# Moving the right-hand SBUF buffers of a float32r attention-and-two-MLPs kernel by 64 and 128 bytes

## The chip, the core and the metric

The kernel is one program on one core of a Trainium2 chip. The metric is the device time of one execution in microseconds (us); lower is better. The time before is 800.19 us, the median of three runs (800.11 to 800.76).

## The reference, cut to what matters

```
# attention over 32 memory slots, 4 batches x 8 heads, 576 rows, head size 64
a      = softmax(phi)                               # phi: b h 576 32
k_m, v_m = a^T k, a^T v                             # b h 32 64
attn   = softmax(q k_m^T / 8);  x = attn v_m        # x: 2304 x 512
# first MLP, d_ff 1536                                second MLP, d_ff 2048
y = ((x w_a) * (x w_b)) w_out                       out = elu(y w_in) w_out2     # 2304 x 512
```

The weights arrive as float64 and are rounded to float32 on the chip. A float32 product is done as three float32r products of a high and a low part each (high x high, high x low, low x high).

## The kernel before, in words

Everything stays in SBUF; TensorE (PE) runs one long, fixed stream of products. A "moving" operand streams through PE, a "stationary" operand is loaded ahead of it by a weight load (PEld). In the built program `matmul(out, w, x)` has `w` stationary and `x` moving. One weight load goes with every product.

The stages, in order:

- **Attention**, about the first 65 us: loads of phi, k, v and q, transposes, scores and softmax, in plain float32 (L376 to L493).
- **ab** (`steps_ab`, L625): 1152 float32r products, 288 columns each. Stationary is `u` (the memory values already multiplied by the weights, made by `step_u`, L513), moving are the attention weights `xhi`, `xlo`.
- **o1** (`steps_o1`, L652): 864 float32r products of 384 columns. Stationary are the weight parts `ulh`, `ull`, moving are the hidden values `gh`, `gl`. ab and o1 alternate from about 91 to 392 us. A run of o1 is 4 column blocks (`for c in range(KC)`), each over a list of hidden blocks `fs`, each with 3 pairs of parts x 2 halves. The last hidden block (the key `own`) has weight tiles of its own in another pool (`pb`, in `to_hi`).
- **h** (`step_h`, L750): 1152 float32r products of 384 columns; stationary `ush`, `usl`, moving `yh`, `yl` of one of three row blocks t = 0, 1, 2.
- **o2** (`steps_o2`, L795): 864 float32r products of 512 columns. Here the activations `g2h`, `g2l` (named `gh`, `gl` in the code) are stationary and the weights `ulh`, `ull` move. h and o2 alternate from 392 us to the end.

VectorE (DVE) and ScalarE (ACT) evacuate PSUM, split values in high and low parts, and convert the weights in pieces (`fill`) beside each step. GpSimd (POOL) issues weight loads, SyncE (SP) the rest.

Pools are taken from two sides of SBUF. Those opened with `side="right"` (`rim`, `py`, `p0`, `pl`, `pb`, `pd`) are stacked from the upper end downwards in the order in which they are opened, each tile in whole units of 32 bytes per partition; the others (`conv`, `pa`, `pu`, `pc`) from the lower end upwards. `edge` (L272) is the first tile at the right, so all tiles of the right side lie below it; `parity` (L292) lies in `p0`, below `y` and above what is opened later.

Of the kernel before, what the change touches and what calls it, by code (L numbers as in the profile page):

```python
# [7 lines left out]
F32 = mybir.dt.float32  # L8
# [13 lines left out]
def attention_then_two_mlps(ctx, tc, q, kv, kv_left, phi, w_ab, w_o1, w_i2, w_o2, out):  # L22
# [14 lines left out]
    B, P, KC, S = q.shape  # L37
# [233 lines left out]
    es_u = ExitStack()  # L271
    pu = es_u.enter_context(tc.tile_pool(name="pu", bufs=2, reuse_waits="tile"))  # L272
    rim = ctx.enter_context(tc.tile_pool(name="rim", bufs=1, side="right", reuse_waits="tile"))
    edge = rim.tile([P, 8], F32, name="edge")
    es_y = ExitStack()
    py = es_y.enter_context(tc.tile_pool(name="py", bufs=1, side="right", reuse_waits="tile"))
    y = [py.tile([P, KC * TB], F32, name=f"y{i}") for i in range(NB)]
# [3 lines left out]
    p0 = es_0.enter_context(tc.tile_pool(name="p0", bufs=2, side="right", reuse_waits="tile"))  # L281
# [7 lines left out]
    ident = p0.tile([P, P], F32, name="ident", bufs=1)  # L289
    rest = pl.tile([P, LEFT, 2], F32, name="rest", bufs=1)  # L290
    a_left = pl.tile([P, 2, P], F32, name="a_left", bufs=1)
    parity = p0.tile([P, 2], F32, name="parity", bufs=1)  # L292


    st = {}
# [599 lines left out]
```

## Time and profile before

| | |
|---|---|
| median of 3 runs | 800.19 us (800.11 to 800.76) |
| the profiled execution | 800.3 us, of which the span from first to last instruction is 798.6 us |
| TensorE's mean granted clock | 0.999 of full speed |
| PE / PEld busy | 779.9 us (98%) / 720.0 us (90%) |
| DVE / ACT busy | 588.9 us (74%) / 398.3 us (50%) |

The profile is one execution. PE's durations of single products overlap, since the products are pipelined; the pace of a stream is therefore read from the starts of its rows, or from a piece of the chain of waits divided by its count. The chain of waits follows the work that ended last back from the end.

### The profile page before, as it was taken

The numbers are of one execution on the slowest core, as the hardware profiler recorded it, in microseconds if no ns is written. First come the engines' busy times: TensorE is split into PE (matmuls) and PEld (weight loads), VectorE is DVE, ScalarE is ACT, GpSimd is POOL, SyncE is SP. The second block draws the span as 40 slices with busy tenths as digits, with TensorE's granted clock in tenths as the row PEclk, the third lists the DMA queues.
The fourth block names the chain that finished last, engine by engine and source line by source line (L and its number), as shares of the span: only waits on it lengthen the run. The fifth ranks groups of instructions, "written<-read, shape, count | busy, mean of one in ns | idle before, by whom it ended". The sixth has DMA issues, their size and how long they took to land.

```text
span 798.6 us, 12970 instructions
## 1 busy us (share of the span) xinstructions
PE 779.9 (98%) x5420; PEld 720.0 (90%) x5420; DVE 588.9 (74%) x924; ACT 398.3 (50%) x616; POOL 38.2 (5%) x83
## 2 busy tenths in 40 slices
PE   5899999999999999999999999999999999999997
PEld 4788899999999999999998988998889988999896
DVE  5798985887787787787997327777977779676464
ACT  5555774543363335333686536554565445653350
POOL 2000000000000000000000000000000000000000
PEclk9999999999999999999999999999999999999999
DMA  9960222121212221121001000111111111000006
GB/s 340 408 268 27 64 97 75 36 76 55 80 33 74 62 71 54 53 78 55 27 27 54 26 1 27 53 53 53 54 47 34 53 53 54 27 1 0 1 1 237
DMA packets 17066, 57.71 MB, mean 72 GB/s; under 512 B 1776, under 2 KB 1776, under 8 KB 17008
## 3 DMA queue, kind: packets, MB, share of 16 engines
q0 software_dynamic: 8784, 31.99, 12.4%
q1 hardware_dynamic: 8224, 24.91, 8.0%
q8 instruction: 42, 0.69, 0.3%
q14 instruction: 16, 0.13, 0.1%
HBM read 52.17 MB, written 4.72 MB: 71 GB/s over the span
## 4 chain that ended last, share of the span: by engine, by line
PE 91%; DMA 4%; DVE 3%; ACT 1%; issue 0%; SPq 0%; DVEq 0%; ACTq 0%
PE o_ps L795 25%; PE h_ps L750 25%; PE o_ps L652 18%; PE ab_ps L625 18%; DMA y<-in_q_dram 3%; PE u_ps L513 3%; PE sc L438 1%; DMA kv_t<-in_kv_dram 1%; DVE ssm L476 0%; PE pk L399 0%; DVE y L481 0%; DVE u L524 0%; PE tp_x L489 0%; DVE gl L636 0%; PE sl L442 0%
## 5 line engine op out<-in xcount | busy, mean ns | idle before, releaser
L625 PE MATMUL ab_ps<-xhi,u 128*128 128x288 f32 x768 | 138.2, 296 | 0.0
L625 PEld LDWEIGHTS ab_ps<-xhi,u 128*128 128x128 f32 x768 | 113.6, 188 | 6.0 <-ACT gh L635 3.7
L795 PE MATMUL o_ps<-ulh,g2h 128*128 128x512 f32 x288 | 113.7, 395 | 0.0
L795 PE MATMUL o_ps<-ull,g2h 128*128 128x512 f32 x288 | 113.6, 394 | 0.0
L770 DVE SCALAR_TENSOR_TENSOR e<-e,th 128x768 f32<-128x768 f32 x48 | 45.8, 954 | 78.4 <-ACT e L767 78.4
L795 PE MATMUL o_ps<-ulh,g2l 128*128 128x512 f32 x288 | 103.0, 395 | 0.0
L750 PE MATMUL h_ps<-yh,usl 128*128 128x384 f32 x384 | 97.8, 335 | 0.0
L750 PE MATMUL h_ps<-yl,ush 128*128 128x384 f32 x384 | 97.7, 335 | 0.0
L750 PE MATMUL h_ps<-yh,ush 128*128 128x384 f32 x384 | 97.6, 335 | 0.0
L761 ACT ACTIVATE e<-h_ps 128x768 f32<-128x768 f32 x48 | 38.9, 811 | 93.6 <-PE h_ps L750 93.1
L625 PE MATMUL ab_ps<-xlo,u 128*128 128x288 f32 x384 | 81.5, 294 | 0.0
L652 PE MATMUL o_ps<-gh,ulh 128*128 128x384 f32 x288 | 74.0, 338 | 0.6 <-ACT ulh L146 0.6
L652 PE MATMUL o_ps<-gh,ull 128*128 128x384 f32 x288 | 73.9, 338 | 0.0
L652 PE MATMUL o_ps<-gl,ulh 128*128 128x384 f32 x288 | 73.9, 337 | 0.0
L632 ACT ACTIVATE a_sb<-ab_ps 128x576 f32<-128x576 f32 x48 | 31.3, 653 | 79.8 <-PE ab_ps L625 79.8
L750 PEld LDWEIGHTS h_ps<-yh,ush 128*128 128x128 f32 x384 | 69.6, 188 | 1.3
L750 PEld LDWEIGHTS h_ps<-yh,usl 128*128 128x128 f32 x384 | 69.4, 188 | 0.0
L750 PEld LDWEIGHTS h_ps<-yl,ush 128*128 128x128 f32 x384 | 69.3, 188 | 0.0
L795 PEld LDWEIGHTS o_ps<-ulh,g2l 128*128 128x128 f32 x288 | 54.0, 187 | 13.2
L795 PEld LDWEIGHTS o_ps<-ulh,g2h 128*128 128x128 f32 x288 | 54.0, 187 | 12.6
L795 PEld LDWEIGHTS o_ps<-ull,g2h 128*128 128x128 f32 x288 | 54.0, 187 | 12.5
L634 DVE TENSOR_TENSOR a_sb<-a_sb,ab_ps 128x576 f32<-128x576 f32 x48 | 36.0, 752 | 36.8 <-PE ab_ps L625 36.4
(95 smaller groups left out, 1291.2 us busy)
## 6 DMA issues: line engine op xcount, KB each, us to landing
raw<-in_w_o_dram POOLq DMA_DIRECT2D x27, 512.0 KB, 3.8
raw<-in_w_ab_dram POOLq DMA_DIRECT2D x18, 512.0 KB, 3.8
kv_t<-in_kv_dram SPq DMA_DIRECT2D x16, 512.0 KB, 10.2
raw<-in_w_i_dram POOLq DMA_DIRECT2D x16, 512.0 KB, 3.8
y<-in_q_dram SPq DMA_DIRECT2D x8, 576.0 KB, 10.2
out_dram<-y SPq DMA_DIRECT2D x8, 512.0 KB, 2.9
raw<-in_w_ab_dram SPq DMA_DIRECT2D x6, 512.0 KB, 9.2
phi_t<-in_phi_dram SPq DMA_DIRECT2D x3, 576.0 KB, 9.9
```

The source lines that it names most:

```text
L438: nc.tensor.matmul(sc[:, u, j * P:(j + 1) * P], qs[u][:, t, j * P:(j + 1) * P], kt[:, u, t * P:(t + 1) * P], start=(t == 0), stop=(t == 1))
L513: nc.tensor.matmul(ps[j:j + M, o, k * 256:k * 256 + 256], vt[r, 2 * k + c, 2 * p + o], w[r, c * 256:c * 256 + 256], start=True, stop=True, ...
L625: nc.tensor.matmul(ps[:, h, 0:HS], u[:, kk, w, n * P:n * P + P], x[b][:, kk, h * HS:(h + 1) * HS], start=(kk == 0 and i == 0), stop=(kk == ...
L632: nc.scalar.activation(out=a_sb, in_=ps[:, :, 0:HS], func=AF.Copy)
L634: nc.vector.tensor_tensor(out=a_sb, in0=a_sb, in1=ps[:, :, 0:HS], op=ALU.mult)
L652: nc.tensor.matmul(ps[:, h, 0:HB], w[:, cc], g[:, h * HB:(h + 1) * HB], start=(n == 0 and i == 0), stop=(n == len(fs) - 1 and i == 2),)
L750: nc.tensor.matmul(ps[:, h, 0:HB], w[:, c], x[:, c, h * HB:(h + 1) * HB], start=(c == 0 and i == 0), stop=(c == KC - 1 and i == 2),)
L761: nc.scalar.activation(out=e, in_=ps[:, :, 0:HB], func=AF.Relu, scale=-1.0)
L770: nc.vector.scalar_tensor_tensor(out=e, in0=e, scalar=1.0, in1=th, op0=ALU.add, op1=ALU.mult)
L795: nc.tensor.matmul(ps[:, k, :], g[:, c * P:(c + 1) * P], w, start=(f == fs[0] and i == 0), stop=(f == fs[-1] and i == 2),)
```

## The change

`edge` grows from 8 to 24 float32 (32 to 96 bytes per partition), and `parity` becomes the first two columns of a tile of 34 (32 to 160 bytes with rounding). Tiles between the two (`y`, and the small softmax tiles, which lie below `y`) move down by 64 bytes, and all right-hand tiles under `parity` by 64 + 128 = 192.

```
-    edge = rim.tile([P, 8], F32, name="edge")
+    edge = rim.tile([P, 24], F32, name="edge")
...
-    parity = p0.tile([P, 2], F32, name="parity", bufs=1)
+    parity = p0.tile([P, 34], F32, name="parity", bufs=1)[:, 0:2]
```

No instruction is added, removed or moved on any engine; two become wider (the memset and the exponential of `edge`, 8 to 24 columns). What changes is where operands begin. The start addresses in the built programs, modulo 256 bytes, as (moving, stationary):

```
products                                count   before        after
ab  L625  xhi,xlo / u, first halves       576   (0|128, 128)  the same
ab  L625  xhi,xlo / u, second halves      576   (128|0, 128)  the same
o1  L652  gh,gl / ulh,ull                 792   (64, 128)     (128, 128)
o1  L652  the same, block "own"            72   (64, 64)      (128, 128)
h   L750  yh,yl / ush,usl, t = 0, 1       768   (128, 128)    the same
h   L750  the same, t = 2                 384   (192, 128)    (128, 128)
o2  L795  ulh,ull / g2h,g2l               864   (128, 192)    (128, 128)
attention, u (float32): ident/y (64,192)->(128,128); y/y (192,192)->(128,128);
  kv/a (64, 192|64)->(128, 0|128); pick in y/m (192,64)->(128,128); ush/vt: the same
```

In ab the two row halves of a product are 1152 bytes apart, so its moving operand alternates between 0 and 128; in the other streams a slice keeps the residue of its tile. Modulo 512 the moved right-hand tiles of o1, h and o2 begin at 384 afterwards, and the left-hand ones at 128, as before.

## Rows read from the trace of the kernel before

**Rows 1.** The page, busy time by engine, and the granted clock by slices.
```profile
PE 779.9 (98%) x5420; PEld 720.0 (90%) x5420; DVE 588.9 (74%) x924; ACT 398.3 (50%) x616; POOL 38.2 (5%) x83
PEclk9999999999999999999999999999999999999999
```

**Rows 2.** The page, chain of waits: shares by engine and by line.
```profile
PE 91%; DMA 4%; DVE 3%; ACT 1%; issue 0%; SPq 0%; DVEq 0%; ACTq 0%
PE o_ps L795 25%; PE h_ps L750 25%; PE o_ps L652 18%; PE ab_ps L625 18%; DMA y<-in_q_dram 3%; PE u_ps L513 3%; PE sc L438 1%; DMA kv_t<-in_kv_dram 1%; DVE ssm L476 0%; PE pk L399 0%; DVE y L481 0%; DVE u L524 0%; PE tp_x L489 0%; DVE gl L636 0%; PE sl L442 0%
```

**Rows 3.** Engines by stretch, from 110 us on; columns in the first row.
```profile
core 0: us, PE busy (x) PEld busy (x) DVE busy (x) ACT busy (x) POOL busy (x), PEclk, DMA share, GB/s
110.00:392.00 282.00, 282.00 (x2308) 273.61 (x2307) 218.10 (x368) 123.75 (x209) 17.40 (x32) 1.00 0.19 61
392.00:768.00 376.00, 376.00 (x1907) 341.22 (x1906) 263.10 (x365) 205.11 (x276) 12.63 (x23) 1.00 0.10 33
```

**Rows 4.** Waits of PE's weight loads after 110 us: total, times, longest.
```profile
PEld ab_ps L625 <- ACT gh L635: 3.7, 9, 0.4
```

**Rows 5.** The chain in order of time: start, us, what.
```profile
131.64 9.36 PE ab_ps L625 x72
...
152.81 12.71 PE o_ps L652 x72
...
376.45 3.18 PE ab_ps L625 x24
...
446.58 12.50 PE h_ps L750 x72
...
475.88 12.51 PE h_ps L750 x72
...
488.39 12.59 PE o_ps L795 x54
...
500.99 12.53 PE h_ps L750 x72
...
513.52 12.60 PE o_ps L795 x54
```

**Rows 6.** Timeline of PE, last o1 runs for t = 1 and 2.
```profile
379.48 0.51 PE L652 MATMUL o_ps<-gh,ulh 128*128 128x384 f32 x2
...
383.64 0.52 PE L652 MATMUL o_ps<-gh,ulh 128*128 128x384 f32 x2
...
384.70 0.51 PE L652 MATMUL o_ps<-gh,ulh 128*128 128x384 f32 x2
...
385.74 0.52 PE L652 MATMUL o_ps<-gh,ulh 128*128 128x384 f32 x2
```

**Rows 7.** Timeline of PE, last o1 run for t = 0: start, us, what.
```profile
363.69 0.51 PE L652 MATMUL o_ps<-gh,ulh 128*128 128x384 f32 x2
...
365.77 0.51 PE L652 MATMUL o_ps<-gh,ulh 128*128 128x384 f32 x2
...
366.81 0.52 PE L652 MATMUL o_ps<-gh,ulh 128*128 128x384 f32 x2
...
368.93 0.51 PE L652 MATMUL o_ps<-gh,ulh 128*128 128x384 f32 x2
...
369.97 0.52 PE L652 MATMUL o_ps<-gh,ulh 128*128 128x384 f32 x2
```

**Rows 8.** Timeline of PE, first and last pair of an early o1 stretch.
```profile
99.65 0.51 PE L652 MATMUL o_ps<-gh,ulh 128*128 128x384 f32 x2
...
105.55 0.51 PE L652 MATMUL o_ps<-gh,ull 128*128 128x384 f32 x2
```

**Rows 9.** The instructions on edge: min/median/max ns, first and last start.
```profile
L528 POOL MEMSET edge<- x1: 105/105/105, 0.7 to 0.7; 128x8 f32 x1
L529 ACT ACTIVATE edge<-edge x1: 209/209/209, 2.0 to 2.0; 128x8 f32<-128x8 f32 x1
```

**Rows 10.** The chain in order of time, its DMA pieces at the start.
```profile
2.58 6.51 DMA kv_t<-in_kv_dram
9.11 11.96 DMA y<-in_q_dram
21.09 9.76 DMA y<-in_q_dram
```

## The prediction

> **What bounds the kernel now.** I read the page first. PE is busy 98% of the span and its clock is granted in full, the 2.4 GHz level, in every slice [rows 1]. The chain of waits says that this busy time is also the path: PE holds 91% of it, and 86% is four streams of products, o2 25%, h 25%, o1 18%, ab 18% [rows 2]. The table by stretches shows that from 110 us to 768 us PE has no gap, while DVE is busy 218.1 of 282.0 us and ACT less [rows 3]; the waits of the weight loads in that time are nine of at most 0.4 us, all in ab, 3.7 us in total [rows 4]. So the time is a sum of counts times paces, and the reader must look at the pace, the time from one product's start to the next. The mean durations do not give it, since products overlap.
>
> The chain's pieces give the paces [rows 5]:
> - ab, 288 columns: 9.36 us / 72 = 130.0 ns.
> - h, 384 columns: 12.50, 12.51 and 12.53 us / 72 = 173.6 to 174.0 ns.
> - o1, 384 columns: 12.71 / 72 = 176.5 ns.
> - o2, 512 columns: 12.59 and 12.60 / 54 = 233.2 to 233.3 ns.
>
> h and o1 have the same number of columns and the same shapes, yet o1 is 2.5 to 2.9 ns slower. 130.0 / 288 = 0.451 ns per column, and 0.451 x 384 = 173.3: ab and h lie on one line, o1 lies over it. The same line at 512 columns gives 231.1, and o2 lies 2.2 ns over it. The two streams over the line are the ones whose moving address minus stationary address is 192 modulo 256. On the line are differences of 0 (h, t = 0 and 1) and 64 (h, t = 2); ab mixes 0 and 128.
>
> **Does the address do it?** The kernel holds its own experiment. In the last o1 runs the block "own" has its weights in the right-hand pool, so (64, 64) products stand between (64, 128) products of the same line, shape and time. For t = 1 there are 24 products at (64, 64), from 379.48 to 383.64 us: 4.16 us / 24 = 173.3 ns. Then come, for t = 2, six at (64, 128), from 383.64 to 384.70: 1.06 / 6 = 177; six at (64, 64) to 385.74: 1.04 / 6 = 173 [rows 6]. For t = 0, twelve at (64, 128) from 366.81 to 368.93 take 2.12 / 12 = 176.7, the next six at (64, 64) 1.04 / 6 = 173.3 [rows 7]. The pace follows the address pair, back and forth within a microsecond, and equal residues sit on the line.
>
> One thing speaks against a simple rule. The first twelve of that run, 363.69 to 365.77, are (64, 128) too and take 2.08 / 12 = 173.3 [rows 7], and in an early run the 34 products from 99.65 to 105.55 take 5.90 / 34 = 173.5 [rows 8]. So (64, 128) can run on the line if the stream enters it in step, and mostly does not; after each (64, 64) block it fell off again. I take the difference as something that makes the slow step possible, and equality as something that removes it.
>
> **The Trainium skill against this.** "TensorE: Matmul & The Clock Gate", section "Step-by-step: what each phase is for", says that PE reads its streaming operand and its weights through two independent ports, so loading the next weights takes no bandwidth from the running product. By it no start address would matter and the sum would be 0, 800.3 us in the profiled execution. The 177 and 173 ns of [rows 6] disagree.
>
> **The change part by part.**
> 1. o1 to (128, 128). Of 864 products, 72 are at (64, 64) already. Of the 792 at (64, 128), 12 are seen on the line in [rows 7], and 36 (those 34 and the last two) in the early run of [rows 8]. That leaves 744 x (176.5 - 173.3 = 3.2 ns) = 2.4 us. Bounds: 0, and 792 x 3.7 (the slowest six of [rows 6]) = 2.9.
> 2. o2 to (128, 128). 864 x (233.3 - 231.1 = 2.2 ns) = 1.9 us. No row shows 512 columns at equal residues; the 231.1 is an estimate, the line through ab and h. Bounds: 0 if 233.3 is what 512 columns take anyway, and 864 x 3.2 = 2.8 if o1's whole step goes. I take 1.9, because o2 has o1's difference of 192 and is over the line as o1 is.
> 3. h, t = 2, from (192, 128) to (128, 128): 0. Its pace is on the line now, and so is that of t = 0 and 1. The runs differ by 0.03 us [rows 5]; 16 steps of t = 2 give at most some 0.3 us either way.
> 4. ab and u have both operands on the left: 0. Attention's float32 products change residues, but before 65 us PE is not the limit; 0, and 0.5 us either way.
> 5. The exponential of `edge` (209 ns) and the memset (105 ns) get 16 more columns [rows 9]; both lie before 2.3 us, while the chain goes on with the k/v load until 9.1 us [rows 10]. 0. If the cover were gone, they could cost no more than their own length again, 0.3 us.
> 6. Loads into right-hand tiles move their SBUF address from 64 or 192 to 128. The chain holds 6.51 + 11.96 + 9.76 = 28.2 us of them [rows 10]. Nothing in the trace shows a load's price by address. The nearest rows are the two pieces for q, which differ by 2.2 us at one and the same residue, so the ends are 2.2 us either way; I take 0, since a move by whole 64 bytes changes neither the count nor the size of the packets.
>
> What is late next? PE stays the path: DVE has 282.0 - 218.1 = 64 us free where o1 gives 2.4, and the waits of [rows 4] are at most 0.4 us each, so at most a few tenths come back there.
>
> Sum: 2.4 + 1.9 = 4.3 us. The profiled execution took 800.3 (span 798.6 and 1.7 around it), 0.1 over the median of 800.19. 800.19 - 4.3 = 795.9 us.
>
> **The rivals.**
> - *Only o1 gains.* Then 233.3 ns belongs to 512 columns and not to the address. For: o2 holds the same 233.2 to 233.3 in both of its runs in [rows 5], whereas o1 shows two paces, and 512 is no multiple of 96 while 288 and 384 are, so a pace that goes by steps could round up. Against: o2 sits over the line with o1's difference. 800.19 - 2.4 = 797.8 us.
> - *Nothing changes.* The pace in o1 is set by the phase in which a stream begins, and the new pair, which lies 256 and not 0 apart modulo 512 (384 and 128), leaves o1 and o2 where they are. For: the same pair shows two paces [rows 7, 8]. Against: the switches within the last runs go with the address [rows 6, 7]. 800.2 us. The skill's rule above would give the same time.
> - *More.* o2's step goes whole (2.8), and h's runs of 12.51 and 12.53 all become 12.50 or less, some 0.5: 800.19 - 2.4 - 2.8 - 0.5 = 794.5 us.
> - *Slower.* Products at (384, 128) modulo 512 collide where none did. ab shows that a stream can get slower at unmoved addresses: 3.18 / 24 = 132.5 instead of 130.0 ns [rows 5], 1.9%. If h, t = 2, takes 1.9% more (384 x 3.3 = 1.3 us) and o2 too (864 x 4.4 = 3.8) while o1 stays, the time is 805.3; with h alone 801.5. It decides from the point where h and o2 lose 1.6 us more than o1 gives. Against: h at (128, 128) is on the line.
>
> **How the numbers follow.** Both o1 and o2 gain: 0.50 (795.9, its own range 795.2 to 796.8). Only o1: 0.25 (797.8, within 0.5). More: 0.07. Nothing: 0.11. Slower: 0.07. A measurement of this kernel can tell 0.2%, 1.6 us, from no change, so faster means under 798.6: the first three, 0.82. Same, 0.11; slower, 0.07. The range must take in the first two cases and most of the third: 794.6 to 798.5.
>
> **What would show it.** In the profile after, every o1 run of 72 in the chain should read 12.48 to 12.50 us instead of 12.71; o2's runs of 54 should read 12.48 instead of 12.60 (12.60 still, if only o1 gains); h for all t 12.50; ab 9.36 as now; the first 65 us the same within 0.5. The prediction is wrong if o1 still reads 12.7, or if ab or h grow.

## The result, and the profile after

The changed kernel takes 793.65 us, the median of five runs (793.42 to 794.12), against 800.19 before (five runs, 799.52 to 800.76): ratio 0.9918, 95% interval 0.9907 to 0.993. The direction was forecast; the size was not. The forecast was 795.9 us with a range from 794.6 to 798.5, and the time lies 0.95 us below the range.

The page of the changed kernel, busy time by engine, answers to [rows 1]:

```profile
PE 773.4 (98%) x5420; PEld 719.1 (91%) x5420; DVE 588.7 (74%) x924; ACT 398.2 (50%) x616; POOL 38.1 (5%) x83
```

PE's busy time fell by 6.5 us, and no other engine's by more than 0.9: the same work, at another pace. PE stays the path. In the table by stretches it has no gap (first fence, columns as in [rows 3]), and the waits of the weight loads in ab are again nine of at most 0.4 us, 3.7 in all (second fence, as [rows 4]):

```profile
110.00:392.00 282.00, 282.00 (x2312) 273.63 (x2311) 219.29 (x369) 123.64 (x209) 17.35 (x32) 1.00 0.19 61
392.00:768.00 376.00, 376.00 (x1926) 345.00 (x1925) 266.26 (x368) 207.69 (x280) 12.60 (x23) 1.00 0.10 33
```

```profile
PEld ab_ps L625 <- ACT gh L635: 3.7, 9, 0.4
```

The chain in order of time (start, us, what) answers to [rows 5]:

```profile
53.37 3.77 PE sc L438 x32
...
81.00 9.79 PE ab_ps L625 x72
...
130.83 9.59 PE ab_ps L625 x72
...
152.13 12.50 PE o_ps L652 x72
...
390.80 24.96 PE h_ps L750 x144
...
444.59 12.50 PE h_ps L750 x72
...
473.45 12.50 PE h_ps L750 x72
485.96 12.28 PE o_ps L795 x54
498.24 12.50 PE h_ps L750 x72
510.74 12.28 PE o_ps L795 x54
```

Per product, o1 went from 176.5 to 12.50 / 72 = 173.6 ns, o2 from 233.3 to 12.28 / 54 = 227.4, h is at 173.6 in its runs of 72, and ab right behind o1 went the other way, from 130.0 to 9.59 / 72 = 133.2. Three pieces of the chain of before, with those above, give the ledger:

```profile
53.95 3.77 PE sc L438 x32
...
81.59 9.79 PE ab_ps L625 x72
...
392.20 25.03 PE h_ps L750 x144
```

| stretch | before | after | less |
|---|---|---|---|
| start to 81 us (attention) | 81.59 | 81.00 | 0.6 |
| ab and o1, up to the first h | 310.6 | 309.8 | 0.8 |
| h, o2 and the end of the span | 406.4 | 401.1 | 5.3 |
| span | 798.6 | 791.9 | 6.7 |

Of the 5.3, o2 is 864 x 5.9 ns = 5.1. In the middle stretch o1 gave 2.2 us (nine runs of 12.71 now at 12.48 to 12.50, and two shorter steps), and ab took 1.5 back: 456 products stand directly behind an o1 run, at 3.3 ns more each.

### The profile page after: what moved, and what is told of

Its sections match the earlier page's. It is cut to its first block, busy times and chain, and to the rows that moved or that the text cites. A ratio compares the mean times of both kernels' runs of the same rounds, so it can differ in the third digit from the quotient of the medians.

```text
span 791.9 us, 12970 instructions
## 1 busy us (share of the span) xinstructions
PE 773.4 (98%) x5420; PEld 719.1 (91%) x5420; DVE 588.7 (74%) x924; ACT 398.2 (50%) x616; POOL 38.1 (5%) x83
## 4 chain that ended last, share of the span: by engine, by line
PE 90%; DVE 4%; ACT 1%; issue 0%; DVEq 0%; ACTq 0%
PE h_ps L750 25%; PE o_ps L795 25%; PE ab_ps L625 19%; PE o_ps L652 18%; PE u_ps L513 3%; PE sc L438 0%; DVE y L465 0%; DVE ssm L476 0%; DVE smx L464 0%; DVE a L181 0%; DVE y L481 0%; DVE u L524 0%; DVE gl L636 0%; DVE ush L201 0%; DVE xlo L70 0%
## 5 line engine op out<-in xcount | busy, mean ns | idle before, releaser
L795 PE MATMUL o_ps<-ulh,g2h 128*128 128x512 f32 x288 | 112.0, 389 | 0.0
```

The costliest lines, as they stand in the source:

```text
L795: nc.tensor.matmul(ps[:, k, :], g[:, c * P:(c + 1) * P], w, start=(f == fs[0] and i == 0), stop=(f == fs[-1] and i == 2),)
```

## The experiments

**One tile at a time.** Each half of the change alone.

```
 edge_only:    edge = rim.tile([P, 24], ...)          parity as before
 parity_only:  parity = p0.tile([P, 34], ...)[:, 0:2]   edge as before
```

Edge alone:

> The kernel before with the wider edge tile alone: y and all tiles below move by 64 bytes, so o2 stands at (128, 128), h for t = 2 at (128, 128), and o1 at (0, 128), a difference of 128. Theory A (a weight load costs a product a fixed 13.3 ns at equal residues, and a step of 3.3 or 6.7 ns more where the residues differ badly): o2 at 227.4 ns as with the whole change, which alone takes 864 x 5.9 = 5.1 us off; o1 has the difference of 128 at which ab shows both paces, so 173.4 to 176.7; total 792.7 to 795.1. Theory B (o2's pace fell for another reason than its own addresses, such as the state in which o1 leaves the stream): o2 stays at 233.3 and the total at 797.8 to 800.2.

Measured: 795.22 us against 799.92, ratio 0.9944 (0.993 to 0.9957). Chain of waits of that kernel:

```profile
130.67 9.60 PE ab_ps L625 x72
...
152.06 12.67 PE o_ps L652 x72
...
487.71 12.28 PE o_ps L795 x54
```

o2 has the whole of its new pace, 227.4 ns, from its own addresses: theory B is out. o1 at (0, 128) is at 12.67 / 72 = 176.0, hardly better than at (64, 128), and ab has lost its 130.0 all the same, so a fast o1 is not what slows ab. Theory A had no such loss in it; the total is 0.1 over its interval.

Parity alone:

> The kernel before with the wider parity tile alone: o1 stands at (192, 128), a difference of 64, its block own at (192, 192); o2 stays at (128, 192) and h as before. Theory A1 (a difference of 64 is as free as 0, as h at t = 2 showed before): o1 at 173.4 ns, 2.4 us less; ab after such an o1 run takes 9.59 us for 72 instead of 9.36, as with the whole change, up to 1.5 us more; total 797.8 to 799.3. Theory A2 (only equal residues are free): o1 at 176.5 and ab at 9.36; total 800.2. Both: o2 at 233.3.

Measured: 799.41 us, ratio 0.999 (0.9982 to 0.9999).

```profile
130.75 9.58 PE ab_ps L625 x72
...
152.13 12.48 PE o_ps L652 x72
...
487.00 12.59 PE o_ps L795 x54
```

A1: o1 at (192, 128), a difference of 64, runs at 12.48 / 72 = 173.3, as fast as at equal residues. A2 is out. ab pays for most of it, and o2 stays. The total is 0.1 over the interval that A1 gave.

So much for nine of the eleven late runs. In the last two, products at (192, 128) and those of "own" at (192, 192) take turns, and they read 12.58 and 12.60 us where before they read 12.61 and 12.56. From the timeline, the first six of "own" in the first of the two take 1.07 / 6 = 178 ns:

```profile
364.37 0.52 PE L652 MATMUL o_ps<-gh,ulh 128*128 128x384 f32 x2
...
365.44 0.51 PE L652 MATMUL o_ps<-gh,ulh 128*128 128x384 f32 x2
```

Two pairs that are fast alone were thus not fast in turn. No run takes this further.

**The pace by itself, by pairs.** A kernel with float32r products alone; in its names, mova to movd and staa to stad begin at 0, 64, 128 and 192 modulo 256.

> A kernel of float32r products alone, nothing of the reference is computed: blocks of 24 products with 512, 384 and 288 columns, for all 16 pairs of a moving and a stationary residue out of 0, 64, 128, 192 modulo 256, once in one order and once in the reverse. Theory A (fixed 13.3 ns per product at equal residues): 226.7, 173.3 and 133.3 ns at each of the four equal pairs, whatever the residue, and at a difference of 192 (moving minus stationary) some 233.3, 176.7 and 136.7. Rival (the pace is proportional to the columns, 0.4514 ns each): 231.1, 173.3 and 130.0 at equal pairs. Rival (the residue 128 itself is good): only the pair (128, 128) is fast. If the two orders differ for one pair, the pace also depends on how the stream enters.

Timeline of PE (start, us, what), blocks of 24 products; the pace is the distance to the next start, divided by 24:

```profile
46.43 5.76 PE L43 MATMUL ps<-mova,stab 128*128 128x512 f32 x24
52.03 5.62 PE L43 MATMUL ps<-movb,stab 128*128 128x512 f32 x24
57.49 5.67 PE L43 MATMUL ps<-movc,stab 128*128 128x512 f32 x24
63.00 5.75 PE L43 MATMUL ps<-movd,stab 128*128 128x512 f32 x24
68.59 5.75 PE L43 MATMUL ps<-mova,stac 128*128 128x512 f32 x24
```

Against a stationary operand at 64, moving operands at 0, 64, 128 and 192 take 233.3, 227.5, 229.6 and 232.9 ns. All 16 pairs fall in these four classes by their difference (192, 0, 64, 128), in both orders; settled, past the first products of a block, equal pairs are at 226.7 at each of the four residues. So at 512 columns it is the difference that counts, not 128. At 384 columns differences of 0 and 64 settle at 173.3 and 128 at 175.9; 192 settles at 173.3 in five of its eight blocks and up to 174.9 in the others, so there the block before has a say, as the expectation put it for pairs whose two orders differ. At 288 columns equal pairs take 131.7 and, settled, none more than 133.4. Of theory A's numbers for equal pairs the first two hold and 133.3 is 1.6 too high; at a difference of 192 its 233.3 holds, but its 176.7 and 136.7 are not seen here. Of the proportional line only 384 columns fit: its 231.1 and 130.0 are out. Each block ran once in each order, in one execution.

**The pace by sizes.**

> A kernel of float32r products alone, nothing of the reference is computed. First equal residues (128, 128) and (0, 128) for 13 sizes from 512 down to 128 columns: theory A has a straight line of slope 1/2.4 ns per column and 13.3 ns at zero columns, until the weight load itself bounds it below some 256 columns; the rival has a line through zero, 0.4514 ns per column, so 202.2 at 448 (A: 200.0) and 144.4 at 320 (A: 146.7). Then 288 columns with the moving operand 1152 bytes apart, as ab has it, for all pairs of residues: with one stationary residue (128) ab showed 130.0 and 133.3; another pair may hold 130.0 always. Then 320 and 256 columns in turn at one residue: 133.3 by A, 130.0 by the rival. Then the moving start in steps of 32 bytes against a fixed stationary one at 512 and 384 columns: by A the slow differences repeat every 256 bytes.

```profile
34.68 5.36 PE L43 MATMUL ps<-movc,stac 128*128 128x480 f32 x24
39.88 5.45 PE L43 MATMUL ps<-mova,stac 128*128 128x480 f32 x24
45.16 5.11 PE L43 MATMUL ps<-movc,stac 128*128 128x448 f32 x24
50.11 5.05 PE L43 MATMUL ps<-mova,stac 128*128 128x448 f32 x24
55.00 4.64 PE L43 MATMUL ps<-movc,stac 128*128 128x416 f32 x24
59.48 4.64 PE L43 MATMUL ps<-mova,stac 128*128 128x416 f32 x24
```

In the rows with movc the residues are equal: 5.20 / 24 = 216.7 ns at 480, 206.3 at 448, 186.7 at 416. From 384 to 512 columns, equal pairs grow by (226.7 - 173.3) / 128 = 0.417 ns a column, one period at the 2.4 GHz level. Less the columns at that rate, 16.7, 19.6 and 13.3 remain; settled blocks of 512, 384, 320 and 256 columns leave about 13.3 as well, 352 leaves 14.7 and 288 11.7. So neither line holds: 13.3 ns over the columns is the common price, with departures, and below 256 columns the pace stays at 111 to 112 ns. Nor are equal residues always the best: with mova, a difference of 128, 448 columns take (55.00 - 50.11) / 24 = 203.8 ns against 206.3, and 352 columns 158.3 against 161.1. With the moving start in steps of 32 bytes against a stationary one at 128, 512 columns are fast at a difference of 0 (226.7) and 64 (228.9) alone; the other six steps take 232.3 to 234.3, and the eight repeat after 256 bytes. At 384 columns that repeat fails: a difference of 160 took 173.7 ns, and 256 bytes further on 176.7. With the two parts of ab, 1152 bytes apart, no pair of the 16 held 130.0; they took 132.0 to 133.3. 320 and 256 columns in turn take 133.3 at equal residues, as theory A had it, and 131.7 at a difference of 64.

**How ab lost.**

> A kernel of float32r products alone, nothing of the reference is computed. 72 products as ab has them (288 columns, moving at 128 and 0 in turn, stationary 128) are entered from 36 products of 384 columns at each of the 16 pairs of residues. Theory C (ab inherits its pace: from o1's slow step it comes into the alternation 128, 132 ns of before, mean 130.0, and from a fast o1 into 131, 131, 132, 140, mean 133.3): after (64, 128) it runs at 130.0, after (128, 128) at 133.3. Rival D (ab's pace of before came from something else beside the products, such as the engines that read PSUM): 133.3 after every entry. Then the same with the stationary operand at 192, 64, 0: from the run of sizes 132.25 at 192 and 64, 133.3 at 0. Then 320 and 256 columns in turn with both moving parts at 128: 131.7 per product against 64 (a difference of 64), 133.3 against 128.

```profile
166.28 6.51 PE L43 MATMUL ps<-movb,stac 128*128 128x384 f32 x36
172.63 25.37 PE L43 MATMUL ps<-movc,stac 128*128 128x288 f32 x180
...
213.66 6.40 PE L43 MATMUL ps<-mova,stad 128*128 128x384 f32 x36
219.90 9.74 PE L43 MATMUL ps<-movc,stac 128*128 128x288 f32 x72
229.48 6.50 PE L43 MATMUL ps<-movb,stad 128*128 128x384 f32 x36
235.82 9.52 PE L43 MATMUL ps<-movc,stac 128*128 128x288 f32 x72
245.17 6.45 PE L43 MATMUL ps<-movc,stad 128*128 128x384 f32 x36
```

The same 72 products take 9.35 / 72 = 129.9 ns behind (64, 192), and 9.58 / 72 = 133.1 behind (0, 192). Behind (64, 128), o1's old pair, it is 129.9 too: the row of 180 joins three blocks over 25.21 us, of which the 36 products of 384 columns at (128, 128) take 6.27 and the last 72 behind them 9.59, so the first 72 have 9.35. Behind the other 14 pairs they take 133.0 to 133.3. Theory C holds in that the entry chooses and ab keeps the state it enters with; rival D is out. But a slow entry alone does not give the fast state, as this stretch shows:

```profile
70.86 6.52 PE L43 MATMUL ps<-movd,staa 128*128 128x384 f32 x36
77.22 9.74 PE L43 MATMUL ps<-movc,stac 128*128 128x288 f32 x72
86.79 6.52 PE L43 MATMUL ps<-mova,stab 128*128 128x384 f32 x36
```

At (192, 0), a difference of 192 as in o1's old pair, the 36 products are as slow, 6.36 / 36 = 176.7 ns (at (64, 128) it is 6.35 / 36 = 176.4), and yet the 72 behind them take 9.57 / 72 = 133. So it is the address pair of the stream in front that counts, in a way that neither its pace nor its difference tells; what in it does so stays open. The whole kernels agree with this table for each entry that they have: 130.0 only behind (64, 128), and 132.5 to 133.3 behind (128, 128), (0, 128), (192, 128) and (64, 64). In the same run the 288 columns against 192, 64 and 0 took 132.1, 132.2 and 133.1, and 320 and 256 in turn 131.6 against 64, 133.1 against 128 and 130.0 against 0. Each entry was run once.

**Better versions.** If ab's loss is an address matter, ab can be moved too. All on the changed kernel:

```
 u_plus64:       + pu.tile([P, 16], F32, name="step", bufs=1)        # ahead of u
 ab_320_256:     + pu.tile([P, 48], F32, name="step", bufs=1)
                 - ps[:, h, 0:HS], ..., x[b][:, kk, h * HS:(h + 1) * HS]
                 + c0, c1 = ((0, 320), (320, S))[h]
                 + wide[:, 192 + c0:192 + c1], ..., x[b][:, kk, c0:c1]   # wide: ps, both banks in one
                 ...                                                # both evacuations read the 576 columns in one piece
 ab_320_256_u0:  the same with pu.tile([P, 32], ...)
```

> The changed kernel once more, beside the next two on one chip: 793.6 us.

> The changed kernel with a pad of 64 bytes ahead of u: u begins at 192, so ab's pairs are (128, 192) and (0, 192), differences of 192 and 64 in turn, instead of 0 and 128. Theory A with the paces of the product-only kernel: ab at 132.25 instead of 133.3 ns, 1152 x 1.1 = 1.2 us less than the changed kernel, 792.4. If ab enters from o1 in another way than there, 791.5 to 794.5.

> The changed kernel with ab's 576 columns cut in 320 and 256 instead of 288 and 288, so that both parts of the moving operand begin at 128, and u at 64 (a pad of 192 bytes): every pair is (128, 64), a difference of 64. The PSUM columns stay in one piece, 192 to 767 of the two banks. Paces of the product-only kernel: 131.7 per product instead of 133.3, 1152 x 1.6 = 1.9 us less than the changed kernel, 791.7. Rival: the reads of PSUM across the two banks cost ACT and DVE more, which PE then waits for: 793.6 or more.

One chip: the changed kernel 794.13 us (ratio to before 0.9921, 0.9906 to 0.9936), u at 192 793.48 (0.9911, 0.9895 to 0.9928), 320 and 256 columns 792.46 (0.9902, 0.9888 to 0.9917). The traces are sharper than the times. Chains of u at 192 and of 320 and 256 columns, one fence each:

```profile
131.27 9.52 PE ab_ps L626 x72
```

```profile
131.45 9.48 PE ab_ps L629 x72
```

9.52 / 72 = 132.2 and 9.48 / 72 = 131.7, both as the product-only kernel said; the differences in time, 0.65 and 1.67 us, are about half and most of the expected 1.2 and 1.9, but the intervals overlap, and they are not told apart by time alone. Of the rival, that reading PSUM across its two banks costs more, nothing shows: the time lies under its 793.6.

> The changed kernel with ab cut in 320 and 256 columns, moving at 128 in both, and u at 0 (a pad of 128 bytes), a difference of 128. In the product-only kernel this pair ran at 130.0 ns after 384 columns at (128, 128), against 131.7 with u at 64: 1152 x 1.7 = 1.9 us less than that version, 790.5. Theory C says that a difference of 128 has two paces and that the entry chooses: where ab is entered from u's products, not from o1, it may fall to 133.3, so that the time is 790.5 to 794.4, and runs of ab right behind o1 read 9.36 us for 72.

> The version with ab cut in 320 and 256 columns and u at 64 once more, beside the one with u at 0: 792.5 us; ab behind o1 at 131.9 ns.

Measured: 792.51 us (0.9907, 0.9893 to 0.992) with u at 0, 792.88 (0.9909, 0.9896 to 0.9923) for the other again. With u at 0:

```profile
131.37 9.36 PE ab_ps L629 x72
142.62 9.82 PE ab_ps L629 x72
164.92 3.12 PE ab_ps L629 x24
169.93 6.59 PE ab_ps L629 x48
```

Behind o1 ab is at 9.36 / 72 = 130.0 again; behind u's products the 48 take 6.59, no better than the 6.58 of the changed kernel. That is what theory C says of a difference of 128: two paces, and the entry chooses. The two versions are equal in time and, by their ratios to before, some 1 to 1.5 us under the changed kernel, about what can be measured.

## Why the prediction was wrong

**Step 2, the gain of o2, is the term that failed: its place was right and its size was not.** The prediction took 231.1 ns for 512 columns, "an estimate, the line through ab and h", and so 1.9 us. o2 was slow by its own addresses, with their difference of 192, and [rows 5] showed it over the line. But the line ran through zero, 0.451 ns per column, and two points at 288 and 384 fixed it. The pair kernel shows that a product of 512 columns at equal residues takes 226.7 ns: 213.3 for its columns at 0.417 ns each, and 13.3 on top, the same 13.3 as at 384 columns. The real gain is 5.9 ns a product, 5.1 us, more than even the prediction's upper bound of 2.8. The point at 288 misled: ab's 130.0 was the pace of an entered state, which [rows 5] had a sign of, 132.5 in the run behind "own"; the prediction used it only for a rival. Where ab entered otherwise it stood at 133.2, and with 173.3 that gives (173.3 - 133.2) / 96 = 0.418 and 226.8 at 512. But this fit would have been luck: 133.2 is not the pace of 288 columns at equal residues, which is 131.7 and by which the same line ends at 228.8. Only a row of 512 columns at equal residues could have told, and the trace of before has none.

**Step 4, ab at 0, failed too,** on the other side and hidden by the first: no address of ab moved, and that was all the reason given; the stream in front of it moved, and ab lost 1.5 us. The prediction had seen that "(64, 128) can run on the line if the stream enters it in step", but did not ask which streams enter from o1. Without this loss the time would have been near 792; it hid part of the first error, and that the time came so near to the range is luck. The chain of the changed kernel shows what the last part of the prediction named as a sign of being wrong, that ab grows.

**Step 1 held.** o1 gave 2.2 us where 2.4 was forecast, and all eleven late runs read 12.48 to 12.50, as written. The (64, 64) products between (64, 128) ones were the right witness.

**Step 3 held:** h gave 0.1 to 0.2, its runs of 72 all 12.50 or 12.51. **Step 5** cannot be seen. **Step 6:** the first 81 us were 0.6 shorter; the same program in its second profile has its scores of the chain at 54.03 instead of 53.37:

```profile
54.03 3.77 PE sc L438 x32
```

The start alone differs by 0.7 us between profiles of one program, so the 0.6 is no effect that can be put down to the change. The three load pieces of the chain sum to 28.8 us in that second profile and to 28.2 before [rows 10], which shows no price by address either way.

**The rivals.** "Only o1" and "nothing" are refuted by o2's 227.4. "Slower" named the pair that lies 256 apart modulo 512, and with it o1 and o2 run at 173.6 and 227.4; its remark that ab can get slower at unmoved addresses is what happened. "More" was the nearest, at 0.07, with its price for o2 too small, and the range, from 794.6, left out even its 794.5. On the Trainium skill's sentence in "TensorE: Matmul & The Clock Gate", "Step-by-step: what each phase is for", that loading weights takes no bandwidth from the running product: the runs here show 226.7 against 233.3 ns for the same product, by where its two operands begin. Whether read bandwidth is what is lost, no run shows.

## What to carry to other kernels

- Where PE is the path and every product has its own weight load, compare the start addresses of the two operands modulo 256: here equal ones were the fastest at 512 columns, where a difference of 192 cost 6.7 ns in 227, and among the fastest at 384. It is no rule for every size: at 448 columns a difference of 128 was faster, 203.8 against 206.3 ns.
- A pace for a size that the trace does not show needs a fixed part and a part per column, fitted on streams known to be in one state. Two points and a line through zero are one assumption too many.
- When a stream's pace is changed, look at the stream behind it, even if nothing of it is touched.

## What the runs showed that was not expected

- The state of a stream lives on: 72 products of one kind took 129.9 or 133.2 ns each, to their end, by the address pair of the 36 products in front of them.
- The pair of a tight ab, two moving parts at 128 and 0 in turn, was faster in that state (130.0) than with equal residues (131.7 at 288 columns).
- Equal residues are no straight line in columns: 448 took 206.3 ns, 19.6 over its columns, while 416 and 512 took 13.3 over theirs. Why that is so, and why the difference of two start addresses sets a pace at all, was not tried.
